# Attention and two MoE layers: conversion of the first MoE's weights, summed by GpSimd in a spare tile in place of an accumulating transfer

## The chip, the cores and the metric

The kernel runs on one core of a Trainium2 chip. The metric is the device time of one execution in microseconds (us). The engines are TensorE (PE; its weight loads are shown as PEld), VectorE (DVE), ScalarE (ACT), GpSimd (POOL) and SyncE (SP), which issues most transfers.

## The reference

Attention with a cumulative bias over q, k, v of 4 batches, 8 heads, 576 positions and 64 columns, then two MoE layers (one expert each) over 2304 tokens of width 512 with 2048 hidden units, all in float32:

```python
scores = scale * np.matmul(q, k.transpose(0, 1, 3, 2))
cum = np.cumsum(np.maximum(s, 0.0), axis=-1)
bias = -(cum[:, :, :, None] - cum[:, :, None, :])
scores = np.where(causal, -1000000000.0, scores + np.minimum(bias, 0.0))
attn = softmax(scores)                       # over the last axis
x = np.matmul(attn, v)                       # laid out as 2304 x 512
h = np.maximum(x @ w_in, 0.0)                # first MoE
x = h * h @ w_out
h = x @ w_in2                                # second MoE
out = (h * np.cos(h)) @ w_out2
```

## The kernel before, in words

The 2304 tokens are worked on in nine blocks of 256 (`NB1`, block number k). For each block the first MoE makes 16 chunks of 128 hidden units (f = 0 to 15): `g1(k, f)` is the product with w_in, `gact` and `grest` the squared ReLU and its split into a high and a low part, `g2(k, f)` the product with w_out. Each `g1` or `g2` is one slot. Attention for the next block runs beside it: `step` handles one attention job (up to 128 queries of one head) and one or two slots. So the order of all instructions is written out by hand, and each engine works through its own list in that order. The second MoE follows when all blocks are done.

Products are split into parts to keep precision, three passes for each product. For the first three blocks (`KC = 3`, k = 0 to 2) the weights of `g1` are two float32 parts, `wt[0, f, 0]` with [:, 0] the high and [:, 1] the low part, in a slot of 512 KB with the tag w{2f}. From k = 3 on `g1` uses two float16 parts, `w16[f]`, with a power of two as scale for each pair of chunks (`wsc1`). The conversion lies in blocks 2 and 3 and is paced by `c_step(t)`, called once a step, where t is the chunk number of the next slot (16 k + f): `c_square` takes the mean square for the scale, `c_add` (L870) adds the two float32 parts, `c_high` (L882) writes the high float16 part on ScalarE, `c_low` (L888) the low one on VectorE in the next step. If `g1(3, f)` comes before its tile is ready, it calls `c_step` until it is.

Before, `c_add` is an accumulating transfer from GpSimd's queue, from [:, 1] onto [:, 0]. `c_high` puts tile 0 in the buffer with the tag p3, tiles 1 and 2 in the slot w0 (the home of the raw weight 0), 3 and 4 in w2, and so on; tile 15 shares w14 with tile 0, which `c_move` (L898) copies there at the end.

The tag p3 is otherwise the third buffer of p. For each job `emit_exp` (L613) makes the softmax's numerators, `emit_split` (L653 to L658) splits them into two float16 parts in p and sends them to pt by a transposing transfer from SP's queue (L633), and `emit_pv` (L699) multiplies pt with v. There are two buffers with the tag p; every third job takes p3 if `p_tile` finds it free. A memset of the tail of p on GpSimd (L653) waits for the same buffer. GpSimd's queue also issues `load_ext` (k<-ext_d, L397), the bias rows that the scores of the next heads need, and `v_load` (L437). Up to block 3 v is split into float16 parts as well (`v_square`, `v_high`, `v_low`, stored by SP in L494). A pool's tile waits until all readers and writers of the tag's previous tile are done.

Of the kernel before, what the change touches and what calls it, by code (L numbers as in the profile page):

```python
# [8 lines left out]
F32 = mybir.dt.float32  # L9
F32R = mybir.dt.float32r  # L10
F16 = mybir.dt.float16
BF16 = mybir.dt.bfloat16
I32 = mybir.dt.int32
ACTF = mybir.ActivationFunctionType
ALU = mybir.AluOpType
# [8 lines left out]
NF = DFF // 128  # L24
# [13 lines left out]
G2LAG = 2  # L38
PASSES = ((0, 0), (0, 1), (1, 0))
KC = 3  # L40
CONV_PACE = 1.8
SQ_A = 12


# [88 lines left out]
def attention_moe_moe_kernel(  # L133
# [18 lines left out]
    nc = tc.nc  # L152
# [5 lines left out]
    wp = ctx.enter_context(tc.tile_pool(name="wp", bufs=1))  # L158
# [4 lines left out]
    at = at_stack.enter_context(tc.tile_pool(name="at", bufs=1, side="right"))  # L163
# [20 lines left out]
    wsc1, hs1, xm = sc1[:, 0:NF // 2], sc1[:, NF // 2:NF], sc1[:, NF:NF + 1]  # L184
# [5 lines left out]
    wt, wst = {}, {}  # L190
# [34 lines left out]
    for x in range(H // 2):  # L225
        t = wp.tile([128, 2, 2 * BT], F32, tag=f"w{2 * NF - (2, 3, 4, 6)[x]}", name="early")
# [27 lines left out]
    def v_own(b):  # L254
# [24 lines left out]
        out=ident, in_=ident, pattern=[[-1, 128]], compare_op=ALU.not_equal, fill=1.0,  # L279
# [23 lines left out]
    def store_ones(eng, n0, n1):  # L303
# [10 lines left out]
        out=mask[:, 384:512], in_=mask[:, 384:512], pattern=[[-1, 128]], compare_op=ALU.is_ge,  # L314
        fill=-8.0e9, base=0, channel_multiplier=1,
    )
    for t in early[2:]:
        early_ones(t, nc.gpsimd)
    nc.vector.tensor_scalar(
        out=cs[0:32, 0:S], in0=cs[0:32, 0:S], scalar1=0.0, scalar2=8.0, op0=ALU.max, op1=ALU.mult  # L320
    )
    cc = []
    for x0, x1, t in ((0, BT, "xh"), (BT, S, "xl")):
        nc.vector.tensor_tensor_scan(
            out=c8[0:32, x0:x1], data0=cs[0:32, x0:x1], data1=cs[0:32, x0:x1],
# [42 lines left out]
    for x in range((XST + 1) // 2):  # L368
        t = wp.tile([128, 2, 512], F32, tag=f"w{2 * NF - 5 - x}", name="xst")
# [18 lines left out]
    lag1, wrest = [], []  # L388
# [207 lines left out]
        j["sb"], j["nb"] = sb, nb[0:r, len(j["ps"]) - 1:len(j["ps"])]  # L596

    def p_tile(i):
        third = nw[2] >= 2 * NF and not wrest and i % 3 == 2 and (0 not in w16 or NF - 1 in w16 and spare[0] is None)
        return at.tile([128, 1280], F16, tag="p3" if third else "p", bufs=1 if third else 2, name="p")  # L600

    def emit_exp(i):
# [32 lines left out]
    def emit_split(i):  # L635
# [8 lines left out]
        if n < EARLY:  # L644
# [4 lines left out]
            yield  # L649
            return  # L650
        p = p_tile(i)
        if cw > w:
            nc.gpsimd.memset(p[0:r, 0:2 * cw].rearrange("p (a c) -> p a c", a=2)[:, :, w:cw], 0.0)  # L653
# [178 lines left out]
    w16, cdone, csum, chigh, clow = {}, [0, 0, 0], [], [], []  # L832
# [11 lines left out]
    def c_scales():  # L844

        while csum:
            f0, f1 = csum.pop(0)
            p = slice(f0 // 2, f1 // 2)
            src = xps[:, BT + 8 + f0:BT + 8 + f1]
            w1s = w1ss[:, c_col(f0):c_col(f1 - 1) + 1]  # L850
            nc.vector.tensor_scalar(out=w1s, in0=src, scalar1=TINY, scalar2=None, op0=ALU.max)
            nc.vector.tensor_tensor(out=hs1[:, p], in0=w1s[:, 0::2], in1=w1s[:, 1::2], op=ALU.add)
            nc.vector.tensor_scalar(
                out=wsc1[:, p].bitcast(I32), in0=hs1[:, p].bitcast(I32), scalar1=24, scalar2=23,
                op0=ALU.logical_shift_right, op1=ALU.logical_shift_left,
            )
            nc.vector.tensor_scalar(
                out=wsc1[:, p].bitcast(I32), in0=wsc1[:, p].bitcast(I32), scalar1=-1, scalar2=205 << 23, op0=ALU.mult,
                op1=ALU.add,
            )  # L860

    def c_square(f):
        junk = m1.tile([128, BT], F32, tag="g", bufs=2, name="wj").bitcast(BF16)
        nc.scalar.activation(
            out=junk, in_=wt[0, f, 0][:, 0].bitcast(F32), func=ACTF.Square, accum_out=w1ss[:, c_col(f):c_col(f) + 1]
        )

    def c_add(f):
        w = wt[0, f, 0]
        nc.gpsimd.dma_start(out=w[:, 0].bitcast(F32), in_=w[:, 1].bitcast(F32), accum_op=ALU.add)  # L870

    def c_high(f):
        w = wt[0, f, 0]
        if f == 0:
            t = at.tile([128, 1280], F16, tag="p3", bufs=1, name="w0")[:, None, 0:1024]
        elif f % 2:
            t = wp.tile([128, 2, 1024], F16, tag=f"w{f - 1}", name="w16")
            spare[0] = t[:, 1:2]
        else:
            t = spare[0]  # L880
        w16[f] = t[:, 0].rearrange("p (a c) -> p a c", a=2)
        nc.scalar.activation(  # L882
            out=w16[f][:, 0], in_=w[:, 0].bitcast(F32), func=ACTF.Copy, scale=wsc1[:, f // 2:f // 2 + 1]
        )

    def c_low(f):
        w = wt[0, f, 0]
        nc.vector.scalar_tensor_tensor(  # L888
            out=w16[f][:, 1], in0=w[:, 0].bitcast(F32), scalar=wsc1[:, f // 2:f // 2 + 1], in1=w16[f][:, 0],
            op0=ALU.mult, op1=ALU.subtract,  # L890
        )

    spare = [None]

    def c_move():

        t = spare[0][:, 0].rearrange("p (a c) -> p a c", a=2)
        nc.gpsimd.dma_start(out=t, in_=w16[0])  # L898
        w16[0] = t
        spare[0] = None  # L900

    def c_step(t, last=None):

        if spare[0] is not None and NF - 1 in w16 and not clow and t > KC * NF:
            c_move()

        for c in clow:
            c_low(c)
        clow.clear()
        while chigh and (chigh[0][1] + 3 <= t or last is not None and chigh[0][0] <= last):  # L910
            c, _ = chigh.pop(0)
            while clow:
                c_low(clow.pop(0))
            c_high(c)
            clow.append(c)
        if last is not None and last in clow:
            for c in clow:
                c_low(c)
            clow.clear()
        c_scales()  # L920
        n = 0
        while cdone[0] < NF and n < 1 and t >= (
            NF + 2 + cdone[0] if cdone[0] < SQ_A else 2 * NF + 2 + 2 * (cdone[0] - SQ_A)
        ):
            c_square(cdone[0])
            cdone[0] += 1
            n += 1
        while cdone[1] < cdone[2] and t >= (KC - 1) * NF + 1 + int(cdone[1] * CONV_PACE):
            c_add(cdone[1])
            chigh.append((cdone[1], t))  # L930
            cdone[1] += 1
# [38 lines left out]
    nw = [2, 0, 0]  # L970
    stq = [(wp, 3)]
    p3 = [0]
# [188 lines left out]
    def g1(k, f):  # L1161
        xh, xl = xb[k]
        if k >= KC and f == 0:
            inverse(xm, xsc[:, k - KC:k - KC + 1])
            inverse(hs1, wsc1)
            nc.vector.tensor_scalar(out=hs1, in0=hs1, scalar1=xm, scalar2=None, op0=ALU.mult)
        if k == KC:
            while f not in w16 or f in clow:
                c_step(k * NF + f, f)
        if k == KC - 1:  # L1170
            cdone[2] = f + 1
        w = w16[f] if k >= KC else wt[0, f, 0]
        hp = hps[:, f % 2, :]
        n = 0
        for c in range(KD):
            for a, e in PASSES:
                nc.tensor.matmul(  # L1177
                    hp, w[:, a, c * 128:(c + 1) * 128], (xh, xl)[e][:, c, :],
                    start=(n == 0), stop=(n == 3 * KD - 1),
                )  # L1180
                n += 1
        gd[k, f] = hp
# [155 lines left out]
    def step(moe=0, bits=0, attn=True):  # L1338
# [34 lines left out]
        if moe and slots and NF < slots[0][1] < (KC + 2) * NF:  # L1373
            c_step(slots[0][1])
# [143 lines left out]
    while prog[0] < unit_done(0):  # L1518
        i = prog[0]
# [3 lines left out]
    for k in range(NB1):  # L1523
# [6 lines left out]
        last = len(slots) - nslots  # L1530
# [444 lines left out]
```

## Time and profile before

| | us |
|---|---|
| median of 3 runs | 1002.06 |
| lowest and highest | 1001.02, 1002.69 |
| the profiled execution | 1003.21 |
| its span | 1001.4 |
| PE busy in the span | 950.5 |
| VectorE, ScalarE, GpSimd busy | 768.0, 728.5, 134.0 |

The span goes from the first to the last instruction of the profiled execution. A line such as L870 is a line of the kernel before. A wait names the instruction that waited and the one whose end released it; for a transfer the releaser is called DMA. An engine that issues a transfer isn't counted as busy, save GpSimd, which prepares its own. The granted clock of PE is 1.00 at 2.4 GHz and 0.50 at 1.2 GHz; a value between is a mean over a stretch.

### The profile page before, as it was taken

To read this page: it belongs to the slowest core of one execution; us is meant where nothing else is said; L and a number is where in the kernel's file an instruction comes from. 1 tells how busy PE (TensorE), PEld (TensorE's weight loads), DVE (VectorE), ACT (ScalarE), POOL (GpSimd) and SP (SyncE) were. 2 spreads that over 40 slices of the span, in tenths; PEclk is the share of its full clock that TensorE was granted. 3 is DMA by queue.
4 is the path that set the end of the run, shared out by engine and by line. 5 is a ranking of instruction groups with operands and counts; after the bars stand their busy time and mean duration, and the time that the engine had idled before them with its cause. 6 is when DMAs were issued, how large, how long until landed. Compare 5 with 4: busy or idle time off the path is not lost.

```text
span 1001.4 us, 21030 instructions
## 1 busy us (share of the span) xinstructions
PE 950.5 (95%) x7474; PEld 736.8 (74%) x7474; DVE 768.0 (77%) x1961; ACT 728.5 (73%) x1736; POOL 134.0 (13%) x235
## 2 busy tenths in 40 slices
PE   6999999898887999999999998999999999999998
PEld 5898898887876898989988998444544455666664
DVE  7899987587666677788899447698778878878775
ACT  7799898686764778878778488577777675665553
POOL 2000111312221011111111004332000000011000
PEclk9999999989997899999999999999999999999999
DMA  8974697949998597558799569611000000012001
GB/s 255 317 255 142 159 204 194 219 104 171 182 159 161 137 183 189 151 147 169 156 198 230 113 254 326 242 43 43 1 1 1 22 1 22 24 67 80 11 33 64
DMA packets 154058, 135.90 MB, mean 136 GB/s; under 512 B 108264, under 2 KB 126000, under 8 KB 153952
## 3 DMA queue, kind: packets, MB, share of 16 engines
q1 hardware_dynamic: 147664, 123.78, 48.5%
q0 software_dynamic: 6288, 10.76, 5.7%
q8 instruction: 59, 0.97, 0.4%
q14 instruction: 47, 0.39, 0.1%
HBM read 89.98 MB, written 15.83 MB: 106 GB/s over the span
## 4 chain that ended last, share of the span: by engine, by line
PE 66%; DVE 10%; DMA 10%; ACT 9%; issue 3%; SPq 1%; DVEq 0%; POOL 0%; ACTq 0%; POOLq 0%
PE o L1683 17%; PE y L1209 13%; PE hps L1177 12%; PE hp L1622 12%; PE bank L1774 5%; DMA pt<-p 4%; DMA rw<-in_w_dram 3%; PE pvs L699 3%; PE qkp L572 3%; ACT sb L613 1%; DMA raw<-in_qk_dram 1%; DVE k L415 1%; DVE sb L590 1%; DMA k<-ext_d 1%; DVE gl L1199 1%
## 5 line engine op out<-in xcount | busy, mean ns | idle before, releaser
L1209 PE MATMUL y<-gh,wt 128*128 128x256 f32 x1152 | 242.7, 294 | 0.0
L1209 PEld LDWEIGHTS y<-gh,wt 128*128 128x128 f32 x1152 | 192.9, 195 | 1.2
L1683 PE MATMUL o<-wt,gh 128*128 128x512 f16 x576 | 171.3, 379 | 1.5 <-ACT gh L1661 1.3
L1209 PE MATMUL y<-gl,wt 128*128 128x256 f32 x576 | 165.6, 287 | 3.9 <-DVE gl L1199 3.9
L1177 PE MATMUL hps<-xh,w 128*128 128x256 f16 x1152 | 146.6, 278 | 10.2 <-DVE w L888 6.2
L1177 PEld LDWEIGHTS <-w 128*128 128x128 f16 x1152 | 107.6, 100 | 28.2 <-DVE w L888 7.0
L1622 PE MATMUL hp<-yh,wt 128*128 128x512 f16 (+1 forms) x448 | 124.9, 348 | 0.0
L1209 PEld LDWEIGHTS y<-gl,wt 128*128 128x128 f32 x576 | 112.4, 195 | 5.3 <-DVE gl L1199 4.8
L1683 PE MATMUL o<-wt,gl 128*128 128x512 f16 x288 | 109.2, 379 | 0.0
L1622 PEld LDWEIGHTS <-wt 128*128 128x128 f16 x672 | 63.9, 98 | 59.1
L1189 ACT ACTIVATE g<-hps,sc 128x256 f32<-128x256 f32 x96 | 45.2, 471 | 76.2 <-PE hps L1177 68.0
L1683 PEld LDWEIGHTS <-gh 128*128 128x128 f16 x576 | 56.3, 98 | 56.4 <-ACT gh L1661 1.6
L613 ACT ACTIVATE sb<-sb 128x128 f32<-128x128 f32 (+7 forms) x152 | 87.4, 575 | 7.7 <-DVE sb L590 7.4
L1177 PE MATMUL hps<-xh,wt 128*128 128x256 f32 x384 | 82.8, 298 | 5.6 <-ACT g L1191 5.5
L654 DVE TENSOR_SCALAR p<-sb 128x384 f16<-128x384 f32 (+3 forms) x120 | 42.9, 358 | 55.6 <-DMA pt<-p 27.8
L1199 DVE TENSOR_TENSOR gl<-g,gh 128x256 fp32r<-128x256 f32 x144 | 61.3, 426 | 27.7 <-ACT gh L1193 14.6
L397 POOL DMA_DIRECT2D k<-ext_d x80 | 43.1, 539 | 271.0 <-ACT g L1192 53.8
L1622 PE MATMUL hp<-yl,wt 128*128 128x512 f16 (+1 forms) x224 | 78.0, 348 | 0.0
L590 DVE CUSTOM_DVE_ANT_0 sb<-qkp,mask 128x128 f32<-128x128 f32 (+7 forms) x152 | 69.2, 456 | 5.4 <-PE qkp L557 3.5
L1177 PEld LDWEIGHTS hps<-xh,wt 128*128 128x128 f32 x384 | 65.5, 198 | 7.5 <-ACT g L1191 6.4
L1647 ACT ACTIVATE a<-kf 128x512 f32<-128x512 f32 (+1 forms) x80 | 46.5, 583 | 31.4 <-DVE kf L1642 30.4
L658 DVE SCALAR_TENSOR_TENSOR p<-sb,p 128x384 f16<-128x384 f32 (+3 forms) x120 | 66.4, 553 | 3.7
(172 smaller groups left out, 2028.0 us busy)
## 6 DMA issues: line engine op xcount, KB each, us to landing
rw<-in_w_dram SPq DMA_DIRECT2D x64, 512.0 KB
raw<-in_qk_dram SPq DMA_DIRECT2D x48, 352.0 KB
yr<-y_d SPq DMA_DIRECT2D x17, 512.0 KB
raw<-in_qk_dram SPq DMA_DIRECT2D x16, 384.0 KB
v_d<-vt SPq DMA_DIRECT2D x16, 320.0 KB
vb<-v_d SPq DMA_DIRECT2D x32, 160.0 KB
vr<-in_v_dram POOLq DMA_DIRECT2D x15, 320.0 KB, 4.7
y_d<-yst SPq DMA_DIRECT2D x18, 256.0 KB
```

What stands on the lines that cost most here:

```text
L397: nc.gpsimd.dma_start(out=hd[n][1][64:68, BT - nq:BT + nl], in_=ext_d[n, :, BT - nq:BT + nl])
L590: nc.vector.tensor_tensor_reduce(out=sb[0:r, c0:c0 + cn], in0=p[0:r, 0:cn], in1=mask[0:r, mo:mo + cn], scale=-0.125, scalar=(3.0e38 if k = ...
L613: nc.scalar.activation(out=sb[0:r, 0:w], in_=sb[0:r, 0:w], func=ACTF.Exp, scale=-1.0, bias=j["nb"], accum_out=z[0:r, ti, x:x + 1],)
L658: nc.vector.scalar_tensor_tensor(out=p[0:r, cw:cw + w], in0=sb[0:r, 0:w], scalar=PSC, in1=p[0:r, 0:w], op0=ALU.mult, op1=ALU.subtract,)
L1177: nc.tensor.matmul(hp, w[:, a, c * 128:(c + 1) * 128], (xh, xl)[e][:, c, :], start=(n == 0), stop=(n == 3 * KD - 1),)
L1189: nc.scalar.activation(out=g, in_=hp, func=ACTF.Relu, scale=hs1[:, f // 2:f // 2 + 1])
L1199: nc.vector.tensor_tensor(out=gl, in0=g, in1=gh, op=ALU.subtract)
L1209: nc.tensor.matmul(yps[k][d // 2][:, d % 2, :], w[:, a, d * 128:(d + 1) * 128], (gh, gl)[e], start=(f == 0 and n == 0 and d % 2 == 0), sto ...
L1622: nc.tensor.matmul(hp, chunk_of(w, a, c), (yh, yl)[e][:, c, :], start=(m == 0), stop=(m == 3 * KD - 1),)
L1647: nc.scalar.activation(out=a, in_=kf, func=ACTF.Sin, scale=-6.2831850)
L1683: nc.tensor.matmul(ops[j][a], (gh, gl)[e][:, a * 128:(a + 1) * 128], w[:, x, :], start=(first and m == 0), stop=(last and m == 2),)
L1774: nc.tensor.matmul(bank[b][:, 0:HB], w[:, a, wx, c * 128:(c + 1) * 128], y_side(j, yx, e, c), start=(start and n == 0), stop=(n == 5), ski ...
```

## The change

`c_add` becomes a GpSimd addition that writes the sum to a tile of its own, `w32[f]`: for f = 0, 1, 2 in the buffer p3, from f = 3 on in the slot w{2f - 2}, the home of the raw weight f - 1, which was summed before. `c_high` and `c_low` read `w32[f]`. Tiles f and f + 1 (f even) go to the slot w{f}, so tile 0 is in its place from the start, and `c_move` is gone. Additions 1 and 2 wait until the low half before them has been written out, since they share p3. The high half comes two chunks after the addition instead of three, and the additions are 1.7 chunks apart instead of 1.8. `p_tile` gives p3 to p before the first addition and once low half 2 is written.

```diff
-CONV_PACE = 1.8
+CONV_PACE = 1.7
...
     def p_tile(i):
-        third = nw[2] >= 2 * NF and not wrest and i % 3 == 2 and (0 not in w16 or NF - 1 in w16 and spare[0] is None)
+        third = nw[2] >= 2 * NF and not wrest and i % 3 == 2 and (cdone[1] == 0 or 2 in w16 and 2 not in w32)
...
     def c_add(f):
         w = wt[0, f, 0]
-        nc.gpsimd.dma_start(out=w[:, 0].bitcast(F32), in_=w[:, 1].bitcast(F32), accum_op=ALU.add)
+        if f < 3:
+            w32[f] = at.tile([128, 640], F32, tag="p3", bufs=1, name="w32")[:, 0:512]
+        else:
+            w32[f] = wp.tile([128, 2, 512], F32, tag=f"w{2 * f - 2}", name="w32")[:, 0]
+        nc.gpsimd.tensor_tensor(out=w32[f], in0=w[:, 0].bitcast(F32), in1=w[:, 1].bitcast(F32), op=ALU.add)
 
     def c_high(f):
-        w = wt[0, f, 0]
-        if f == 0:
-            t = at.tile([128, 1280], F16, tag="p3", bufs=1, name="w0")[:, None, 0:1024]
-        elif f % 2:
-            t = wp.tile([128, 2, 1024], F16, tag=f"w{f - 1}", name="w16")
-            spare[0] = t[:, 1:2]
-        else:
-            t = spare[0]
-        w16[f] = t[:, 0].rearrange("p (a c) -> p a c", a=2)
+        if f % 2 == 0:
+            spare[0] = wp.tile([128, 2, 2, 512], F16, tag=f"w{f}", name="w16")
+        w16[f] = spare[0][:, f % 2]
         nc.scalar.activation(
-            out=w16[f][:, 0], in_=w[:, 0].bitcast(F32), func=ACTF.Copy, scale=wsc1[:, f // 2:f // 2 + 1]
+            out=w16[f][:, 0], in_=w32[f], func=ACTF.Copy, scale=wsc1[:, f // 2:f // 2 + 1]
         )
 
     def c_low(f):
-        w = wt[0, f, 0]
         nc.vector.scalar_tensor_tensor(
-            out=w16[f][:, 1], in0=w[:, 0].bitcast(F32), scalar=wsc1[:, f // 2:f // 2 + 1], in1=w16[f][:, 0],
+            out=w16[f][:, 1], in0=w32.pop(f), scalar=wsc1[:, f // 2:f // 2 + 1], in1=w16[f][:, 0],
             op0=ALU.mult, op1=ALU.subtract,
         )
...
-    def c_move():
-
-        t = spare[0][:, 0].rearrange("p (a c) -> p a c", a=2)
-        nc.gpsimd.dma_start(out=t, in_=w16[0])
-        w16[0] = t
-        spare[0] = None
+    spare, w32 = [None], {}
 
     def c_step(t, last=None):
 
-        if spare[0] is not None and NF - 1 in w16 and not clow and t > KC * NF:
-            c_move()
...
-        while chigh and (chigh[0][1] + 3 <= t or last is not None and chigh[0][0] <= last):
+        while chigh and (chigh[0][1] + 2 <= t or last is not None and chigh[0][0] <= last):
...
-        while cdone[1] < cdone[2] and t >= (KC - 1) * NF + 1 + int(cdone[1] * CONV_PACE):
+        while cdone[1] < cdone[2] and t >= (KC - 1) * NF + 1 + int(cdone[1] * CONV_PACE) and (
+            cdone[1] not in (1, 2) or cdone[1] - 1 in w16 and cdone[1] - 1 not in w32
+        ):
             c_add(cdone[1])
```

## Rows read from the trace of the kernel before

**Rows 1.** The page: busy time by engine, granted clock in 40 slices, chain by engine.
```profile
PE 950.5 (95%) x7474; PEld 736.8 (74%) x7474; DVE 768.0 (77%) x1961; ACT 728.5 (73%) x1736; POOL 134.0 (13%) x235
...
PEclk9999999989997899999999999999999999999999
...
PE 66%; DVE 10%; DMA 10%; ACT 9%; issue 3%; SPq 1%; DVEq 0%; POOL 0%; ACTq 0%; POOLq 0%
```

**Rows 2.** Busy time by window, blocks 1 to 4: PE, PEld, DVE, ACT, POOL; clock, DMA, GB/s.
```profile
110.60:179.50 68.90, 66.15 (x681) 62.98 (x680) 55.79 (x156) 60.24 (x166) 12.53 (x24) 1.00 0.87 198
179.50:257.30 77.80, 68.29 (x613) 63.43 (x613) 55.60 (x202) 57.45 (x166) 17.60 (x36) 0.93 0.78 162
257.30:340.20 82.90, 68.69 (x597) 60.50 (x597) 50.85 (x136) 51.82 (x131) 14.96 (x28) 0.84 0.87 152
340.20:402.00 61.80, 60.07 (x642) 55.94 (x642) 47.57 (x133) 50.04 (x132) 9.22 (x19) 1.00 0.84 190
```

**Rows 3.** Line 870, the accumulating transfers: ns min/median/max, first and last start, landing.
```profile
L870 POOL DMA_DIRECT2D wt<-wt x16: 843/916/1258, 176.9 to 302.2; - x16
...
DMA to landing us min/median/max: 3.5/5.5/11.4
```

**Rows 4.** Timeline of ScalarE at the first high half: start, duration, idle before.
```profile
199.60 0.72 ACT L882 ACTIVATE w<-wt,sc 128x512 f16<-128x512 f32 x1 [5.32 <-DMA k<-ext_d]
```

**Rows 5.** The chain in order of time, blocks 2 and 3: start, us, what.
```profile
225.76 8.26 DMA k<-ext_d
...
261.64 9.64 DMA pt<-p
...
288.93 11.54 DMA pt<-p
...
301.85 8.37 DMA pt<-p
...
327.55 0.67 DVE w L888
```

**Rows 6.** Waits (us, times, longest): block 1, block 2, two of block 3, block 4.
```profile
DVE p L654 <- DMA pt<-p: 2.1, 1, 2.1
...
DVE p L654 <- DMA pt<-p: 7.4, 4, 4.7
...
DVE p L654 <- DMA pt<-p: 17.2, 3, 6.6
...
PE hps L1177 <- DVE w L888: 6.2, 3, 4.8
...
DVE p L654 <- ACT sb L613: 4.8, 6, 1.4
```

**Rows 7.** Timeline of VectorE's writes of p: first and last of eight narrow jobs.
```profile
203.50 0.25 DVE L654 TENSOR_SCALAR p<-sb 64x192 f16<-64x192 f32 x1 [1.35 <-ACT sb L613]
...
222.00 0.21 DVE L654 TENSOR_SCALAR p<-sb 128x128 f16<-128x128 f32 x1
```

**Rows 8.** DMA issues by line: KB each, median us to landing.
```profile
k<-ext_d POOLq DMA_DIRECT2D x48, 11.0 KB, 3.5
```

**Rows 9.** Groups of GpSimd's instructions: busy us, mean ns, idle before.
```profile
L870 POOL DMA_DIRECT2D wt<-wt x16 | 14.6, 955 | 2.2 <-issue 1.9 <-DVE vt L487 0.2
...
L1696 POOL TENSOR_TENSOR wt<-os,wt 128x512 f32<-128x512 f32 x8 | 10.1, 1270 | 287.5 <-ACT os L1695 256.6 <-DVE wt L1720 30.9
```

**Rows 10.** Timeline of GpSimd's and VectorE's instructions near 881 and 883 us.
```profile
881.12 0.42 DVE L1788 TENSOR_TENSOR hs<-bank,hs 128x256 f32<-128x256 f32 x1 [0.52 <-PE bank L1774]
...
882.16 0.69 DVE L1642 TENSOR_TENSOR kf<-kf,a 128x512 f32<-128x512 f32 x1
...
883.18 1.26 POOL L1696 TENSOR_TENSOR wt<-os,wt 128x512 f32<-128x512 f32 x1 [1.33 <-ACT os L1695]
...
883.23 1.76 DVE L1642 TENSOR_TENSOR kf<-kf,a 128x512 f32<-128x512 f32 x1
```

**Rows 11.** Busy time by window, 500 to 525 us.
```profile
500.00:525.00 25.00, 24.00 (x258) 22.02 (x258) 23.07 (x68) 19.09 (x46) 4.30 (x12) 1.00 0.92 199
```

More of the change, by code (lines that the diff above doesn't have):

```diff
@@ L869, in c_add @@
         w = wt[0, f, 0]
-        nc.gpsimd.dma_start(out=w[:, 0].bitcast(F32), in_=w[:, 1].bitcast(F32), accum_op=ALU.add)
-    def c_high(f):
-        w = wt[0, f, 0]
-        if f == 0:
-            t = at.tile([128, 1280], F16, tag="p3", bufs=1, name="w0")[:, None, 0:1024]
-        elif f % 2:
-            t = wp.tile([128, 2, 1024], F16, tag=f"w{f - 1}", name="w16")
-            spare[0] = t[:, 1:2]
-        else:
-            t = spare[0]
-        w16[f] = t[:, 0].rearrange("p (a c) -> p a c", a=2)
+        if f < 3:
[3 more added lines that the diff above has]
+        nc.gpsimd.tensor_tensor(out=w32[f], in0=w[:, 0].bitcast(F32), in1=w[:, 1].bitcast(F32), op=ALU.add)
+    def c_high(f):
+        if f % 2 == 0:
+            spare[0] = wp.tile([128, 2, 2, 512], F16, tag=f"w{f}", name="w16")
+        w16[f] = spare[0][:, f % 2]
         nc.scalar.activation(
-            out=w16[f][:, 0], in_=w[:, 0].bitcast(F32), func=ACTF.Copy, scale=wsc1[:, f // 2:f // 2 + 1]
+            out=w16[f][:, 0], in_=w32[f], func=ACTF.Copy, scale=wsc1[:, f // 2:f // 2 + 1]
         )
     def c_low(f):
-        w = wt[0, f, 0]
         nc.vector.scalar_tensor_tensor(
-            out=w16[f][:, 1], in0=w[:, 0].bitcast(F32), scalar=wsc1[:, f // 2:f // 2 + 1], in1=w16[f][:, 0],
+            out=w16[f][:, 1], in0=w32.pop(f), scalar=wsc1[:, f // 2:f // 2 + 1], in1=w16[f][:, 0],
             op0=ALU.mult, op1=ALU.subtract,
         )
-    spare = [None]
-    def c_move():
-        t = spare[0][:, 0].rearrange("p (a c) -> p a c", a=2)
-        nc.gpsimd.dma_start(out=t, in_=w16[0])
-        w16[0] = t
-        spare[0] = None
+    spare, w32 = [None], {}
     def c_step(t, last=None):
-        if spare[0] is not None and NF - 1 in w16 and not clow and t > KC * NF:
-            c_move()
         for c in clow:
```

## The prediction

> **What bounds the kernel now.** First the page. TensorE (PE) is busy 950.5 of 1001.4 us and holds 66% of the chain of work that ended last [rows 1]. The kernel as a whole is bound by PE, and only a stretch in which PE starves has anything to give. The line of granted clocks shows where that is: nine tenths everywhere but in slices 9, 13 and 14 of 40, that is 200 to 225 and 300 to 350 us [rows 1].
>
> Second, busy time by token block. I cut the span at the evictions of y (ScalarE's copies at 110.6, 179.5, 257.3, 340.2 and 402.0 us), so that each stretch is one block, k = 1 to 4 [rows 2]. Blocks 1 and 4 run at full clock with PE busy 66.15 of 68.9 us (96%) and 60.07 of 61.8 (97%). Block 2 takes 77.8 us at a mean clock of 0.93, block 3 takes 82.9 at 0.84. Blocks 3 and 4 have the same 32 product slots, on float16 weights, in 17 steps each, yet block 3 is 21.1 us longer. The conversion runs in blocks 2 and 3 alone: its adds are issued from 176.9 to 302.2 us [rows 3].
>
> Third, what PE lacks there. ScalarE stands idle for 5.32 us until the first high half at 199.60 [rows 4], and PE's next products wait for it. In the chain a k load takes 8.26 us from 225.76; it is queued on GpSimd behind two accumulating transfers. Transposes (pt<-p) stand in it with 9.64, 11.54 and 8.37 us, and near the end PE waits for a low half that was converted at the last moment [rows 5].
>
> Fourth, the waits by block. VectorE's write of p waits for a transpose to free its buffer: 2.1 us in block 1, 7.4 in block 2, 17.2 in block 3, and in block 4 only for ScalarE [rows 6]. GpSimd's memset of p waits for the same buffers, and k loads stand behind it in GpSimd's queue.
>
> **The change, part by part.** I followed c_step's rules through the steps (it is called once a step, with t the chunk of the next slot). For the kernel before this gives adds in groups of 2, 1, 1, 1, 2 and then singly, as the trace has them.
>
> *The third p buffer (tag p3).* Before, converted tile 0 sits in p3 from its high half to the move at the end of block 3, so jobs 62, 65, ..., 92 (eleven) write p into two buffers instead of three. After, p3 holds the sums of f = 0, 1, 2 until low half 2, and only jobs 56, 59 and 62 lose it. Those have 128 or 64 rows of 192 columns or fewer, and such jobs already ran with two buffers from 203.50 to 222.00 us, eight writes, without VectorE waiting for a transpose (the first and the last in [rows 7]). Block 2's and 3's 24.6 us of such waits over 40 writes make 0.6 us for one; the nine jobs from 56 to 64 would cost 5.5 us by that and nothing by the narrow ones. I take 1.5, near the narrow ones.
>
> *High half 0* no longer goes to p3 but to the slot of its own raw weight, so it has no transpose to wait for: the 5.32 us go. Late next are VectorE and ScalarE themselves, busy 71% and 74% of block 2 [rows 2].
>
> *Accumulating transfers.* Sixteen of 256 KB, 5.5 us to landing, 11.4 at most, and the move go [rows 3]. With them goes what delayed the k load at 225.76: the usual one lands in 3.5 us [rows 8], so about 5 of the 8.26 us. Less DMA may also let transposes land earlier; I count nothing for that.
>
> *The adds on GpSimd.* None in this stretch before; the nearest row is the same operation on the same shape and type near the end, 1270 ns [rows 9]. 16 x 1.27 = 20.3 us replace 14.6 us of issuing [rows 9] on an engine busy 23% of block 2. Behind an add wait k loads, v loads and memsets; add 0 waits for job 53's transpose, adds 1 and 2 for low halves 0 and 1 on VectorE, emitted in the same step, and the next k load comes a step later. Bounds for this queueing: 0, or all of 20.3 - 14.6 = 5.7 us if every difference reached PE. I take 0, since a k load is issued a head ahead of its use.
>
> *What an add does to VectorE.* One add starts at 883.18 us, and the VectorE subtraction that starts at 883.23, with both inputs in SBUF, takes 1.76 us; the same one took 0.69 at 882.16. A VectorE operation with one input in PSUM took 0.42 beside the add of 880.57 [rows 10]. So an add costs VectorE between 0 and 1.07 us, 0 to 17.1 over sixteen. Most VectorE operations of an attention step have both inputs in SBUF, so I take 0.7 x 16 = 11 us. VectorE is busy 106.5 of 160.7 us in the two blocks; elsewhere, at 23.07 of 25 us, PE still kept 24.00 [rows 11]. So most of it hides, and I charge 3 us. The Trainium skill ("SBUF — State Buffer", section "Who interferes with whom") says that a VectorE instruction with two SBUF inputs and a GpSimd instruction that reads SBUF exclude each other, the second waiting out the whole of the first; these rows agree, and with nothing hidden the 3 would be 17.1, which is rival 2.
>
> *Delay from add to high half 3 to 2, pace 1.8 to 1.7.* Before, f = 13 to 15 are converted in the steps just before their product and 15 is forced inside it; low halves cost PE 6.2 us [rows 6]. After, low half 15 comes two steps ahead of product 15, so this goes. ScalarE's and VectorE's instructions keep number and size. High half 4 now waits for low half 3, whose scratch lay in its slot, but that was emitted a step earlier: nothing.
>
> **The sum.** Block 3 becomes block 4 with its own extra work: 61.8 plus 3.3 us (VectorE 50.85 against 47.57, the larger of the two side engines' differences) = 65.1, so 17.8 less. Block 2: PE's busy time times the granted clock, 68.29 x 0.93, is 63.5 us of work; at block 1's 96% that is 66.1, with 1.5 for the early jobs 67.6, so 10.2 less. The lock gives 3 back. Together 25.0 less. The gain stays, since PE is 95% busy over the span. The profiled execution took 1003.21 us, 1.15 above the median of 1002.06; the 978.2 there are 977 against the median.
>
> **The rivals.**
> 1. *The transposes are late because of the DMA engines, not the buffer.* For: DMA share is 0.87 in block 3, with v stores beside the long transposes. Against: block 1 has 0.87 too, with three buffers and 2.1 us of waits. Then only the early stall (some 4.8 us of PE), 5 us of the k load and the late conversions (6.2) go, less 3 for the lock: 13 us, 989.
> 2. *The lock binds*: 17.1 us instead of 3, so 14 of the gain are given back: 991. Against: (106.5 + 17.1) / 135 = 92% of VectorE would still be just below what rows 11 show beside a busy PE.
> 3. *The third buffer doesn't come back*, since its condition also wants the first MoE's weights all read by then: rival 1 without the k load, 994. Against: block 1's few waits.
> 4. *Slower: VectorE ends last.* The transposes stay as they are, and every add pushes a VectorE operation that PE waits for, 17.1 us, with 5.7 us of k loads behind adds, against the 16 us that go even in rival 1: 1002 + 22.8 - 16 = 1009. It decides once VectorE is busy over some 93% of blocks 2 and 3 [rows 11]; with the span unchanged it is 123.6 of 160.7 us, 77%, which speaks against it.
>
> **How the numbers follow.** Forecast 64%, rival 1 19%, rival 2 8%, rival 3 3%, rival 4 5%, no change 1%. A difference under 0.2% can't be told from none here. The cases below 1000 hold 94%; I put faster at 0.92, same at 0.02, slower at 0.06, as the price of an add beside VectorE is the least known. The forecast's own range is 968 to 985: at the low end block 3 equals block 4 (21.1 less) and block 2 runs at 98% (64.8, so 13.0 less); at the high end a third of the gain is missing. Rivals 1 and 2 and some DMA relief that I counted at nothing (3 us) make it 965 to 993.
>
> **What would show it.** Block 3 about 65 us, block 2 about 68, block 4 as it was; clock near 1.0 in both. Writes of p waiting for transposes under 6 us in the two blocks instead of 24.6. No PE wait for low halves. Sixteen GpSimd adds of about 1.27 us, with VectorE operations beside them up to 1.1 us longer. It is wrong if block 3 stays above 75 us, if transposes still lead the chain, or if VectorE is over 93% busy while PE waits for it.

## The result and the profile after

The changed kernel takes 979.51 us (median of 4 runs, 975.83 to 980.61) against 1002.18 for the kernel before: a ratio of 0.9769, 95% interval 0.9742 to 0.9796. That is 22.7 us less; the forecast was 977, 25 less. The profiled execution took 979.24 us, its span is 977.5. The sum came out nearly right, but not its parts.

The page after: busy time by engine, granted clock in 40 slices, chain by engine. It answers to [rows 1].

```profile
PE 939.1 (96%) x7474; PEld 728.4 (75%) x7474; DVE 782.2 (80%) x1961; ACT 728.3 (75%) x1736; POOL 139.9 (14%) x234
...
PEclk9999999999999999999999999999999999999999
...
PE 70%; DVE 12%; ACT 9%; DMA 5%; issue 4%; SPq 0%; DVEq 0%; ACTq 0%
```

The slices below nine tenths are gone, and the transfers' share of the chain fell from 10% to 5%. VectorE is 14.2 us busier with the same number of instructions; that is the first hint at what went otherwise.

Busy time by window, blocks 1 to 4 of the changed kernel (columns as in [rows 2]):

```profile
110.40:179.60 69.20, 66.33 (x683) 63.07 (x681) 56.95 (x156) 60.29 (x167) 12.36 (x23) 1.00 0.88 198
179.60:255.50 75.90, 67.02 (x613) 62.17 (x612) 66.52 (x203) 58.11 (x167) 24.32 (x40) 0.96 0.58 139
255.50:315.90 60.40, 58.60 (x597) 53.35 (x596) 53.19 (x134) 51.02 (x130) 15.18 (x24) 0.97 0.80 166
315.90:377.30 61.40, 60.03 (x642) 55.89 (x642) 47.57 (x133) 49.96 (x131) 9.22 (x19) 1.00 0.87 193
```

Block 3 went from 82.9 to 60.4 us (forecast 65.1), block 2 only from 77.8 to 75.9 (forecast 67.6); blocks 1 and 4 stand. In block 2 VectorE is busy 66.52 us where it was 55.60, and the DMA share fell from 0.78 to 0.58.

Three of the rows before have direct answers: the adds for [rows 3], ScalarE's first high half for [rows 4] and the wait of p's write for a transpose, blocks 2 and 3 together, for [rows 6]. The three views are line 874, the timeline of ScalarE, and the waits (us, times, longest).

```profile
L874 POOL TENSOR_TENSOR w<-wt x16: 1272/1300/1979, 177.3 to 283.2; 128x512 f32<-128x512 f32 x16
```

```profile
188.78 0.72 ACT L880 ACTIVATE w<-w,sc 128x512 f16<-128x512 f32 x1
```

```profile
DVE p L654 <- DMA pt<-p: 0.8, 2, 0.6
```

The first high half runs at 188.78 with no idle time before it, where ScalarE had stood 5.32 us. Writes of p wait 0.8 us instead of 24.6. PE waits for no low half.

What holds block 2 is in its timeline: GpSimd's adds and, beside them, VectorE (start, us, instruction).

```profile
198.68 2.64 POOL L874 TENSOR_TENSOR w<-wt 128x512 f32<-128x512 f32 x2 [1.65 <-ACT k L405]
201.95 1.29 POOL L874 TENSOR_TENSOR w<-wt 128x512 f32<-128x512 f32 x1
...
199.10 0.94 DVE L654 TENSOR_SCALAR p<-sb 128x128 f16<-128x128 f32 x1 [0.29 <-DMA pt<-p]
200.07 1.40 DVE L658 SCALAR_TENSOR_TENSOR p<-sb,p 128x128 f16<-128x128 f32 x1
201.50 1.97 DVE L412 TENSOR_TENSOR hi<-raw,hi 64x192 fp32r<-64x192 f32 x1
...
206.14 0.21 DVE L654 TENSOR_SCALAR p<-sb 128x128 f16<-128x128 f32 x1
206.38 0.29 DVE L658 SCALAR_TENSOR_TENSOR p<-sb,p 128x128 f16<-128x128 f32 x1
...
207.70 0.35 DVE L412 TENSOR_TENSOR hi<-raw,hi 64x192 fp32r<-64x192 f32 x1
```

Beside the three adds from 198.68 to 203.24 three VectorE operations take 4.31 us together; the same three shapes take 0.85 us a few us later, with no add near. In the 10 us from 199.6 VectorE is busy 9.70 and PE 7.23 (columns as in [rows 2]):

```profile
199.60:209.60 10.00, 7.23 (x65) 6.86 (x65) 9.70 (x32) 7.78 (x24) 4.22 (x7) 1.00 0.31 77
```

### The profile page after: what moved, and what is told of

It reads as the page before. It is cut to its first block, busy times and chain, and to the rows that moved or that the text cites. A ratio compares the mean times of both kernels' runs of the same rounds, so it can differ in the third digit from the quotient of the medians.

```text
span 977.5 us, 21019 instructions
## 1 busy us (share of the span) xinstructions
PE 939.1 (96%) x7474; PEld 728.4 (75%) x7474; DVE 782.2 (80%) x1961; ACT 728.3 (75%) x1736; POOL 139.9 (14%) x234
## 4 chain that ended last, share of the span: by engine, by line
PE 70%; DVE 12%; ACT 9%; DMA 5%; issue 4%; SPq 0%; DVEq 0%; ACTq 0%
PE o L1673 18%; PE y L1199 13%; PE hps L1167 13%; PE hp L1612 12%; PE bank L1764 5%; PE qkp L572 3%; PE pvs L699 3%; DMA rw<-in_w_dram 3%; ACT sb L613 1%; DVE k L415 1%; DVE sb L590 1%; DMA pt<-p 1%; DVE gl L1189 1%; ACT g L1182 1%; DMA raw<-in_qk_dram 1%
## 5 line engine op out<-in xcount | busy, mean ns | idle before, releaser
L1199 PE MATMUL y<-gh,wt 128*128 128x256 f32 x1152 | 238.1, 290 | 0.0
L1199 PEld LDWEIGHTS y<-gh,wt 128*128 128x128 f32 x1152 | 189.0, 191 | 1.2
L1199 PE MATMUL y<-gl,wt 128*128 128x256 f32 x576 | 163.1, 283 | 0.5 <-DVE gl L1189 0.5
L1167 PE MATMUL hps<-xh,w 128*128 128x256 f16 x1152 | 143.0, 274 | 3.0 <-ACT g L1179 3.0
L1199 PEld LDWEIGHTS y<-gl,wt 128*128 128x128 f32 x576 | 110.1, 191 | 1.4 <-DVE gl L1189 0.9
L1189 DVE TENSOR_TENSOR gl<-g,gh 128x256 fp32r<-128x256 f32 x144 | 62.1, 431 | 24.5 <-ACT gh L1183 14.9
L658 DVE SCALAR_TENSOR_TENSOR p<-sb,p 128x384 f16<-128x384 f32 (+3 forms) x120 | 68.5, 571 | 3.7
L654 DVE TENSOR_SCALAR p<-sb 128x384 f16<-128x384 f32 (+3 forms) x120 | 47.8, 398 | 28.4 <-ACT sb L613 11.2
```

The costliest lines, as they stand in the source:

```text
L654: nc.vector.tensor_scalar(out=p[0:r, 0:w], in0=sb[0:r, 0:w], scalar1=PSC, scalar2=None, op0=ALU.mult)
L658: nc.vector.scalar_tensor_tensor(out=p[0:r, cw:cw + w], in0=sb[0:r, 0:w], scalar=PSC, in1=p[0:r, 0:w], op0=ALU.mult, op1=ALU.subtract,)
L1167: nc.tensor.matmul(hp, w[:, a, c * 128:(c + 1) * 128], (xh, xl)[e][:, c, :], start=(n == 0), stop=(n == 3 * KD - 1),)
L1189: nc.vector.tensor_tensor(out=gl, in0=g, in1=gh, op=ALU.subtract)
L1199: nc.tensor.matmul(yps[k][d // 2][:, d % 2, :], w[:, a, d * 128:(d + 1) * 128], (gh, gl)[e], start=(f == 0 and n == 0 and d % 2 == 0), sto ...
```

## The experiments

Experiments one to four ran on one chip, five to eight on a second, nine to twelve on a third, and the kernel before ran beside each group: it took 999.75, 999.63 and 999.86 us. A comparison between groups is between chips, so I also compare the sum of blocks 2 and 3 in each profile: 160.7 us before, 136.3 after. Each fence of windows below shows block 2 and block 3 of one kernel (columns as in [rows 2]). Pace is the number of chunks from one addition to the next, delay that from an addition to its high half.

**One: the third buffer, without GpSimd adds.** Theory A is the prediction's: the third buffer first, and adds that cost VectorE time. Theory B is its rival 1. Tile 0 is moved out of p3 right after low half 0 instead of at the end of block 3, and tiles share slots as in the changed kernel.

```diff
-        third = nw[2] >= 2 * NF and not wrest and i % 3 == 2 and (0 not in w16 or NF - 1 in w16 and spare[0] is None)
+        third = nw[2] >= 2 * NF and not wrest and i % 3 == 2 and (0 not in w16 or 2 in w16)
...
+            if f == 1 or f % 2 == 0:
+                spare[0] = wp.tile([128, 2, 1024], F16, tag=f"w{f - f % 2}", name="w16")
+            t = spare[0][:, f % 2:f % 2 + 1]
+        if f == 1:
+            c_move()
```

> The kernel before with one difference: tile 0 leaves p3 by its move right after low half 0, so p has its third buffer back from job 65 on; adds stay accumulating transfers, pace 1.8 and delay 3 stay. Theory A (the third buffer is most of the gain, and the GpSimd adds cost VectorE time in block 2): block 3 falls from 82.9 to 64 to 69 us (late low halves still cost up to 6), block 2 to 70 to 75; total 976 to 988. Theory B (the accumulating transfers' load on the DMA engines made the transposes late, the buffer is second): the transposes stay late, total 993 to 1002.

Measured: 983.48 us, ratio 0.9846 (0.9812 to 0.9880). The sum of the blocks is 140.5.

```profile
180.10:250.00 69.90, 65.67 (x613) 61.21 (x612) 55.47 (x202) 57.18 (x167) 18.93 (x39) 0.98 0.87 184
250.00:320.60 70.60, 59.02 (x597) 53.51 (x596) 50.87 (x136) 51.39 (x130) 13.44 (x25) 0.98 0.94 174
```

So 16 us come from the early move and the third buffer with every transfer still there; B falls as it was put. Theory A has the total, but not the blocks (64 to 69 and 70 to 75): block 3 is still 10.2 us longer than in the changed kernel, block 2 is 6.0 us shorter.

**Two: the adds on VectorE.**

```diff
-        nc.gpsimd.tensor_tensor(out=w32[f], in0=w[:, 0].bitcast(F32), in1=w[:, 1].bitcast(F32), op=ALU.add)
+        nc.vector.tensor_tensor(out=w32[f], in0=w[:, 0].bitcast(F32), in1=w[:, 1].bitcast(F32), op=ALU.add)
```

> The changed kernel with its sixteen adds on VectorE, about 0.69 us each, 11 us in all. Theory A (an add on GpSimd costs VectorE about as much as doing it there, 13 us more VectorE time in the trace): within 3 us of the changed kernel, 976 to 982, VectorE busy about 779. Rival (the longer VectorE operations beside GpSimd adds cost PE nothing, since they fall into VectorE's free time): 982 to 990.

Measured: 970.41 us, ratio 0.9711 (0.9680 to 0.9741). The sum is 126.6.

```profile
179.80:248.80 69.00, 66.24 (x623) 61.65 (x621) 62.08 (x212) 57.67 (x167) 11.53 (x31) 0.98 0.62 153
248.80:306.40 57.60, 56.59 (x592) 51.93 (x589) 53.69 (x142) 50.43 (x130) 7.40 (x18) 1.00 0.90 173
```

Both expected times were missed on the other side (VectorE's busy time, 777.6 us in all, came as expected): VectorE does the whole add itself, in 0.685 us each, and the kernel is faster by 9 us (9.7 by the sums). VectorE is busy 115.8 us in the two blocks, against 119.7 with the adds on GpSimd.

**Three: GpSimd writes, but reads nothing** (each sum of weights is left out, a constant stands in its place).

```diff
+        nc.gpsimd.memset(w32[f], 0.03)
```

> The changed kernel with each GpSimd add replaced by a memset of the same tile (the weights' sum is left out): GpSimd reads nothing. Theory A (the add blocks VectorE operations with two inputs in SBUF, and that holds block 2 at 75.9 us): VectorE busy falls by 10 to 13 us, block 2 to 67 to 70, total 970 to 974. Rival (block 2 is held by jobs 56 to 64 with two p buffers and by the V preparation): VectorE busy falls, block 2 stays over 74, total 977 to 980.

Measured: 968.96 us, ratio 0.9694 (0.9665 to 0.9722). The sum is 125.1.

```profile
180.70:246.90 66.20, 64.08 (x613) 59.78 (x612) 56.55 (x203) 57.74 (x168) 15.80 (x40) 1.00 0.66 153
246.90:305.80 58.90, 57.20 (x597) 52.31 (x596) 49.94 (x135) 50.55 (x129) 10.19 (x24) 1.00 0.93 176
```

VectorE's busy time in the two blocks falls by 13.2 us and the blocks by 11.2, most of it in block 2 (75.9 to 66.2): theory A, by a little more than it said. A memset is also shorter than an add (0.54 us against 1.3), so the 11.2 us hold more than the price of held VectorE operations; they bound that price from above. VectorE's groups in the two blocks show which operations were held (busy, mean ns, idle before); first the changed kernel:

```profile
L658 DVE SCALAR_TENSOR_TENSOR p<-sb,p 128x128 f16<-128x128 f32 (+6 forms) x40 | 21.2, 531 | 1.2
L654 DVE TENSOR_SCALAR p<-sb 128x128 f16<-128x128 f32 (+6 forms) x40 | 18.0, 449 | 7.1 <-ACT sb L613 2.5 <-ACT k L405 1.7 <-issue 1.3
L885 DVE SCALAR_TENSOR_TENSOR w<-w,sc,w 128x512 f16<-128x512 f32 x16 | 14.3, 896 | 0.0
```

and here the one that only writes:

```profile
L658 DVE SCALAR_TENSOR_TENSOR p<-sb,p 128x128 f16<-128x128 f32 (+6 forms) x40 | 19.2, 479 | 1.2
L654 DVE TENSOR_SCALAR p<-sb 128x128 f16<-128x128 f32 (+6 forms) x40 | 13.6, 339 | 9.7 <-ACT sb L613 4.5 <-DMA pt<-p 3.3 <-POOL p L653 0.9
L885 DVE SCALAR_TENSOR_TENSOR w<-w,sc,w 128x512 f16<-128x512 f32 x16 | 11.9, 744 | 1.7 <-ACT w L880 1.7
```

The 4.4 us of L654 are those of an operation with one input, so the two-input rule that the prediction cited is not the whole of it. The same section of the Trainium skill ("SBUF — State Buffer", "Who interferes with whom") also counts tensor_scalar among the operations that, under conditions on their operands, can run in a mode that takes the port pair shared with GpSimd; L654, at 449 ns beside adds and 339 beside memsets, agrees.

**Four: the changed kernel with two buffers of p.**

```diff
-        third = nw[2] >= 2 * NF and not wrest and i % 3 == 2 and (cdone[1] == 0 or 2 in w16 and 2 not in w32)
+        third = nw[2] >= 2 * NF and not wrest and i % 3 == 2 and (cdone[1] == 0 or NF - 1 in w16 and NF - 1 not in w32)
```

> The changed kernel, but p3 stays closed to p until all sixteen tiles are converted, as before. Theory A: writes of p wait for transposes again, block 3 back to 73 to 80 us, total 990 to 1000. Theory B (less DMA traffic is what matters): block 3 at most 65 us, total 979 to 984.

Measured: 979.04 us, ratio 0.9800 (0.9768 to 0.9831). The sum is 136.4.

```profile
179.50:250.20 70.70, 65.20 (x630) 60.69 (x629) 63.19 (x203) 57.79 (x168) 23.82 (x38) 1.00 0.62 149
250.20:315.90 65.70, 59.51 (x582) 54.04 (x580) 56.27 (x135) 50.87 (x129) 16.42 (x26) 0.95 0.77 154
```

Theory A as I had put it falls here: closing the third buffer again costs 5.3 us in block 3 and gives 5.2 in block 2, so nothing in all. The third buffer is not needed in the changed kernel. Theory B has the total, with block 3 0.7 us over its bound. That left pace and load open (theory A2: two buffers are late only beside the transfers).

**Five: early move with the new pace and delay, adds still transfers** (experiment one's edit and these two lines).

```diff
-CONV_PACE = 1.8
+CONV_PACE = 1.7
...
-        while chigh and (chigh[0][1] + 3 <= t or last is not None and chigh[0][0] <= last):
+        while chigh and (chigh[0][1] + 2 <= t or last is not None and chigh[0][0] <= last):
```

> The kernel before with the early move (as the run that took 983.5) and the changed kernel's pace 1.7 and delay 2. Theory A2 (the late low halves cost PE 4.7 us there, the rest of its distance to 969 is the accumulating transfers' load): 978 to 982, no PE wait for low halves in block 3. Rival (with delay 2 ScalarE meets transfers that have not landed, 11.4 us at most against 5.5 in the middle): ScalarE waits for transfers and the time is 983 to 990.

Measured: 971.52 us, ratio 0.9736 (0.9699 to 0.9772). The sum is 127.6, against 140.5 at the old pace.

```profile
180.50:247.60 67.10, 64.35 (x614) 59.91 (x614) 55.60 (x201) 57.85 (x168) 18.92 (x39) 1.00 0.92 187
247.60:308.10 60.50, 57.60 (x597) 52.43 (x596) 50.58 (x137) 50.76 (x130) 13.27 (x25) 1.00 1.13 204
```

That is twelve us for two constants (eight by experiment eleven, the same kernel again), 6.5 below the nearer of the two expectations, and that at a DMA share of 1.13 in block 3. In this execution the load didn't hold the block up; experiment eleven shows one in which it did.

**Six: the changed kernel at the old pace and delay** (1.8 and 3).

> The changed kernel with pace 1.8 and delay 3 as before. If the late low halves cost their 6 us still: 983 to 987, with PE waiting for low halves in block 3. If an add of 1.3 us in place of a transfer of 5.5 to 11.4 us makes pace and delay matter less: 978 to 981.

Measured: 988.82 us, ratio 0.9893 (0.9857 to 0.9929), 1.8 us over the first expectation. The sum is 145.7. PE waits for low halves again (waits of block 3):

```profile
PE hps L1167 <- DVE w L885: 5.3, 4, 1.8
```

```profile
179.90:253.20 73.30, 66.08 (x614) 61.17 (x613) 63.14 (x202) 57.16 (x167) 22.00 (x39) 0.98 0.59 141
253.20:325.60 72.40, 62.31 (x597) 55.38 (x596) 57.22 (x136) 51.64 (x131) 16.47 (x25) 0.93 0.66 144
```

The waits are 5.3 us, but block 3 grows by 12.0; its clock falls from 0.97 to 0.93 and PE is busy 3.7 us longer on the same products.

**Seven: adds on VectorE, two buffers** (experiments two and four together).

> Adds on VectorE (970.4 with three buffers) and p3 closed to p until all tiles are converted. Theory A2 (two buffers are late only beside the accumulating transfers; without them the third is worth little): 970 to 975, writes of p waiting for transposes under 8 us in blocks 2 and 3. Theory A as first put (the third buffer is the gain, and only the GpSimd adds hid that in the run with two buffers): 980 to 990.

Measured: 973.55 us, ratio 0.9751 (0.9719 to 0.9784). The sum is 130.7, 4.1 more than with three buffers. A2's numbers hold: writes of p wait 4.3 us for transposes (it said under 8), and without transfers and without GpSimd adds the third buffer is worth about 3 us, though the intervals of the two runs overlap.

**Eight: adds on VectorE, with other transfers in place of the accumulating ones.**

```diff
...
+        nc.gpsimd.dma_start(out=load_d[f], in_=wt[0, f, 1].bitcast(F32))
```

> Adds on VectorE (970.4), and after each a transfer of 512 KB from SBUF to a scratch in DRAM on GpSimd's queue, sixteen in all, at the places of the accumulating ones; nobody waits for them. Theory A2 (the load on the DMA engines and the queue costs time even with three buffers): 974 to 982, transposes and k loads on the chain again. Rival (only the late low halves and the move set 983.5 apart from 970.4): 969 to 972.

Measured: 978.29 us, ratio 0.9787 (0.9751 to 0.9824). The sum is 134.5, 7.9 more than without them. In block 3 PE itself waits for a transpose (waits):

```profile
PE pvs L700 <- DMA pt<-p: 3.3, 1, 3.3
```

So load beside the transposes can cost time with three buffers, as A2 said. These stores have twice the bytes of an accumulating transfer, but the packets of GpSimd's queue took less of the DMA engines' span than in experiment five (5.1 against 5.8%; 2.4 with neither, in experiment two):

```profile
q0 software_dynamic: 6208, 14.69, 5.1%
...
q0 software_dynamic: 6288, 10.76, 5.8%
```

So the 7.9 us are these stores' price; they neither give nor bound that of the accumulating transfers.

**Nine: pace and delay alone, on the kernel before.**

> The kernel before with pace 1.7 and delay 2 alone; p3 stays with tile 0 to the end, adds stay transfers. Theory C (pace and third buffer take away different waits, 12 us and 16 us where the other edit is absent or present alike): 986 to 990, writes of p waiting for transposes as before. Rival (with conversions early enough two buffers do, as they did without transfers, 973.5): 972 to 979.

Measured: 984.11 us, ratio 0.9859 (0.9818 to 0.9901). The sum is 142.1.

```profile
181.50:255.00 73.50, 66.07 (x613) 61.38 (x612) 55.62 (x201) 58.01 (x167) 18.22 (x37) 0.98 0.87 175
255.00:323.60 68.60, 60.47 (x597) 54.44 (x596) 50.66 (x138) 51.08 (x130) 14.44 (x27) 0.95 1.00 176
```

The two waits of p's writes, block 2 and block 3:

```profile
DVE p L654 <- DMA pt<-p: 10.4, 6, 3.2
...
DVE p L654 <- DMA pt<-p: 14.5, 3, 7.2
```

This is just below theory C's range, and the run to learn from: writes of p wait 24.9 us for transposes, as in [rows 6], and yet 16 us are gone. PE's busy time in block 3 fell from 68.69 [rows 2] to 60.47 us on the same products, as its granted clock rose from 0.84 to 0.95. Those waits were not a measure of what PE lost.

**Ten and eleven: the changed kernel, and transfers in its place, on one chip.**

> The changed kernel, for a comparison on one chip: 976 to 981, block 2 some 75 us.

> Early move, pace 1.7, delay 2 with accumulating transfers (971.5 on another chip). Theory C (an add on GpSimd costs more than the transfer it replaces): 6 to 9 us below the changed kernel, 970 to 973. Rival (the 8 us were the chip's): within 3 us of it.

Measured: 979.54 us (977.26 to 980.31) with GpSimd adds and 975.70 (973.60 to 977.78) with transfers; ratios 0.9808 (0.9772 to 0.9843) and 0.9773 (0.9736 to 0.9810). The medians differ by 3.8 us, less than theory C's 6 and more than its rival's 3; four of the six runs with transfers lie below all six with adds, while the intervals of the two ratios overlap. So the swap alone gains nothing here, and rather costs 4 us (8 with experiment five's 971.52). The blocks, first of the changed kernel, then of the one with transfers:

```profile
179.50:254.10 74.60, 67.27 (x613) 62.42 (x613) 66.23 (x203) 58.36 (x167) 23.93 (x40) 0.95 0.59 141
254.10:315.10 61.00, 58.51 (x597) 53.88 (x596) 54.43 (x134) 51.03 (x129) 15.10 (x24) 0.97 0.81 165
...
179.90:247.30 67.40, 64.32 (x614) 59.95 (x613) 54.47 (x198) 57.75 (x168) 18.55 (x37) 1.00 0.92 181
247.30:314.40 67.10, 59.62 (x597) 54.16 (x596) 51.37 (x139) 50.70 (x129) 13.61 (x27) 0.95 1.08 188
```

With transfers block 2 is 7.2 us shorter. Block 3 is 6.1 longer in this profile, and 6.6 longer than in experiment five, whose kernel it is. A transpose stands in its chain with 16.20 us, and PE waits for a transpose (chain, then waits of block 3):

```profile
273.27 16.20 DMA pt<-p
...
PE pvs L699 <- DMA pt<-p: 6.8, 1, 6.8
```

So one kernel with three buffers has executions in which a transpose is late and others in which PE hardly waits for one (0.6 us in experiment five). The one profiled here, at 977.78 us, is the longest of its six.

**Twelve: transfers for tiles 0 to 8, VectorE for 9 to 15,** with the early move and the new pace and delay.

```diff
...
+        if f < 9:
+            nc.gpsimd.dma_start(out=w[:, 0].bitcast(F32), in_=w[:, 1].bitcast(F32), accum_op=ALU.add)
+            w32[f] = w[:, 0].bitcast(F32)
+            return
+        w32[f] = wp.tile([128, 2, 512], F32, tag=f"w{2 * f - 4}", name="w32")[:, 0]
+        nc.vector.tensor_tensor(out=w32[f], in0=w[:, 0].bitcast(F32), in1=w[:, 1].bitcast(F32), op=ALU.add)
```

> As the run before, but tiles 9 to 15 are summed by VectorE into a tile of their own, so transfers are left in block 2 only. From the blocks of the two parents (67.1 us of block 2 with transfers, 57.6 of block 3 with VectorE adds): 967 to 969. If the blocks don't add up so: 970 to 973.

Measured: 968.73 us (967.59 to 969.05), ratio 0.9702 (0.9664 to 0.9740). The sum is 125.1. The blocks add up as expected: transfers where they cost least (block 2), adds on VectorE where transfers made a transpose late (block 3).

```profile
179.20:246.70 67.50, 64.63 (x621) 60.22 (x620) 56.56 (x204) 57.74 (x168) 19.10 (x39) 1.00 0.88 192
246.70:304.30 57.60, 56.60 (x593) 51.94 (x590) 53.30 (x141) 50.35 (x130) 7.54 (x18) 1.00 0.97 177
```

On one chip it is 10.8 us faster than the changed kernel, and as short as the run that left the adds out.

## Why the prediction was right, and where it was not

*The place and the size of the whole: right.* All of the gain lies in blocks 2 and 3 (24.4 us), later blocks only move forward, the clock rises, the early ScalarE stall and PE's waits for low halves go. The prediction put that stall down to a transpose, its own row [rows 4] to a k load; which it was stays open.

*The lock: mis-sized.* I put 0.7 us of VectorE on an add, 11 in all, of which 3 on the path. VectorE's busy time rose by 13.3 us in the two blocks, and memsets in place of the adds shorten them by 11.2. The argument that it hides took 23.07 of 25 us elsewhere [rows 11] as the ceiling over a stretch of 135 us; but the adds cluster. Nine start in block 2, three of them within 4.6 us, and there VectorE was busy 9.70 of 10 us while PE waited: the prediction's own sign of being wrong, in one stretch. Rival 2 had the mechanism, that the price doesn't hide; its 17.1 us are more than the 11.2.

*The third buffer: the step that failed.* I made it the first cause, by the waits of p's writes. With GpSimd adds it is worth 0, with VectorE adds 3. The early move, which frees it beside the transfers, is worth 16 us at the old pace, and 8 at the new one (984.11 to 975.70). It was one of two ways to the same time. Rival 1 had the other half, that the DMA engines' load makes transposes late: with two buffers writes of p wait 24.9 us for them beside transfers (experiment nine) and 4.3 without (seven).

*Pace and delay: mis-sized.* I counted PE's 6.2 us of waits. The two constants alone give 16 us on the kernel before and 9 on the changed one (988.82 to 979.5). Part of that is the clock: in block 3 of the kernel before, at a granted clock of 0.84 [rows 2], PE's products took 8.2 us more busy time than at the new pace, at 0.95. How the rest splits between late halves, the steps behind them and the transposes was not taken apart.

*Accumulating transfers against adds: the wrong sign.* I had 5 us for a k load and a price of 3. The gain of 2 that this leaves was not there: on one chip the kernel with transfers is 3.8 us shorter (it also moves tile 0 through p3 instead of summing there, and the intervals overlap). What carries the change is what came with it, not what names it.

*Why the sum held.* Block 3 fell by 4.7 us more than forecast and block 2 by 8.3 less, with 3 of that in the forecast's lock. That these two misses cancel to less than 1 us is luck. I had modelled block 3 on block 4, an undisturbed block with the same slots. That size stood (60.4 against 61.4 us), while the 3.3 us that I put on it for VectorE's extra work did not show. Block 2 misses by the price of the adds, 9.7 us there by experiment three.

*Open.* Why the changed kernel's block 2 is 5.2 us shorter with two buffers than with three, at 3.3 us less VectorE time, was not tried. The traces show that other operations meet the adds. In the changed kernel two small ones, L727, stand in the chain beside the add at 239.75 with 1.64 us, where the same two took 0.14 at 216.22 with no add near, and PE loses time and clock there after 8.26 busy us of the 10 before:

```profile
216.22 0.14 DVE z L727 x2
...
239.41 1.64 DVE z L727 x2
...
239.60:249.60 10.00, 7.36 (x52) 6.75 (x53) 8.29 (x23) 5.33 (x13) 1.57 (x3) 0.66 0.57 112
```

With two buffers the add there meets another operation (L1189), and PE is busy without a gap at a clock of 1.00 from 239.5 to the end of the block. Whether the buffer or chance decides what meets what is not shown.

## What to carry to other kernels

Take the size of a disturbed stretch from an undisturbed one with the same work, as block 3's from block 4; what the change itself brings into the stretch, as the adds in block 2, has to be priced on top. Don't add up waits: several can stand for the same lost time. Here the early move alone and the two constants alone each returned 16 us of the 24 to 28 that both return together. Before an operation goes to GpSimd beside a busy VectorE, price it as if VectorE did it, per cluster and not over the mean: here VectorE needs 11.0 us for the sixteen adds, GpSimd's adds cost it 13.3, and doing them on VectorE was 9 us faster. When an edit brings a schedule change with it, time the schedule change alone.

## What the runs showed of the hardware

An add on GpSimd held VectorE operations of several sizes: one on 128x128 took 1.40 instead of 0.29 us, one with a single SBUF input 0.94 instead of 0.21, two on 128x2 1.64 instead of 0.14. The add itself took up to 1.98 us (median 1.30). GpSimd memsets of the same tile held none to speak of: L654's mean in the two blocks was 339 ns with them, 449 with the adds and 329 in the kernel before, with neither. With accumulating transfers beside it, the same kernel's block 3 took 60.5 us in one execution and 67.1 in another, with a transpose of 16.20 us in the chain.
